# Split attention: ScalarE's work for coming heads and its copies of sums are queued behind a step's exp and its rounded transposed probabilities

## The chip, the cores and the metric

One core of a Trainium2 chip runs the whole program. The metric is the device time of one execution in microseconds (us). TensorE does the matrix products, VectorE, ScalarE and GpSimd the work on elements, and SyncE's queue starts the DMA transfers. In views of the profile they are PE (with PEld, its weight loads), DVE, ACT, POOL and SP. Every engine takes its own instructions strictly in the order of the program.

## The reference, cut to what matters

Attention over 4 sequences of 576 positions with 8 heads of 64, a causal window of 128 positions and a linear bias by distance, and then two MLPs on its output of 2304 tokens by 512:

```python
scores = scale * np.matmul(q, k.transpose(0, 1, 3, 2))
bias = slopes[:, None, None] * (-np.abs(rel).astype(np.float32))[None, :, :]
mask = (rel >= 0) & (rel < window)
scores = np.where(mask, scores + bias[None], -1000000000.0)
attn = np.exp(scores - np.max(scores, axis=-1, keepdims=True))
attn = attn / (np.sum(attn, axis=-1, keepdims=True) + 1e-09)
x = (attn @ v) as (2304, 512)
h = x @ w_in1; g = max(h, (clip(h, -1, 1) + 1)**2 / 4); x = g @ w_out1
h = x @ w_in2; g = h * clip(h + 3, 0, 6) / 6;           y = g @ w_out2
```

## The kernel before

Everything is in fp32, and most products are made from a rounded part and its remainder ("hi" and "lo"): two or three matrix products take the place of one. ScalarE makes the rounded part by a copy (`split_hi`, L152) and VectorE or GpSimd the remainder by a subtraction (`split_lo`, L159).

**Units, heads, steps.** The 2304 tokens are cut into 12 units of 64 to 256 tokens, and a unit has 8 heads, so there are 96 heads, numbered 0 to 95 here. A head has a step for every 128 of its query positions: heads of units with 192 or 256 tokens have two, those of units with 128 tokens one. Units 0 to 3 (heads 0 to 31) run in a plain form ("whole"), units 4 to 11 in the split form that the change is about. Of those, units 5, 7 and 11 have 128 tokens: heads 40 to 47, 56 to 63 and 88 to 95 have one step each, and the heads before them (32 to 39, 48 to 55, 80 to 87) have two.

**A step of split attention.** `stage_a` makes the scores in the one PSUM bank "s" (L411: `kh` and then `kl` against `qs`), overlays the two halves of the window (L438), adds the bias and takes the row's extreme (L441, VectorE), takes exp with its sum (L445, ScalarE), adds epsilon and inverts the sum (L448 and L449, VectorE), and scales (L450, GpSimd). `stage_b` comes three ticks later: a transpose by TensorE (L470), its rounded copy by ScalarE (L152 into `dist` or `tt`), the remainder (L483, VectorE) and two selections by GpSimd (L488). `stage_c`, five ticks after `stage_a`, multiplies with the values (L554), and adds up the halves of the result through ScalarE (`xf`, L152) and VectorE (L572). For odd heads `to_x` then makes the MLP's input `x` (L152 on ScalarE, L159 on VectorE).

**Preparing a head.** `prep(n)` turns the loaded keys and queries of head n into operands: `kh` (L389) and the first half of `qs` (L390) by ScalarE, then `kl` (L391) by VectorE from `kh`, and `qs` (L393) by GpSimd from ScalarE's `qs`; for even heads the values `vs` too. The first score product of head n needs `kh` and the finished `qs`, the second `kl`.

**The order.** `tick()` runs the late stages of earlier steps, then `stage_a` of its own, and then, under `behind()`, the `to_x` of finished pairs and `more_preps`: the step (n, 0) prepares head n+1 where head n has two steps and up to head n+2 where it has one. So head 39 (two steps) prepares 40, and head 40 (one step) prepares 41 and 42. Only SyncE's queue is in the order of the code. On the other engines the framework's scheduler chooses the order, and `tc.issue_after(op)` binds it: what is traced in such a block stands behind `op` on `op`'s own engine. `behind()` names three operations of VectorE: the last row reduction (L441), the last remainder of transposed probabilities (L483) and the last sum (L572). On ScalarE and GpSimd it binds nothing.

**The MLP between the steps.** The first MLP runs in the same stretch. For each of 16 chunks of a block, `first` is 12 matrix products of 256 or 384 tokens (h, L659), `activate` goes VectorE (L688), ScalarE (L689), VectorE (L690), ScalarE (`g`, L152), GpSimd (`g`, L159), and `second` is 12 more products (acc, L701), two chunks late. `run_block` calls `flush` (acc, and at a block's end `finish`, which copies the sums out) under `behind()` too. In wide blocks h has a single bank, so the next h waits for L690.

Of the kernel before, what the change touches and what calls it, by code (L numbers as in the profile page):

```python
# [15 lines left out]
AF = mybir.ActivationFunctionType  # L16
# [13 lines left out]
HI = dict(v="act", th="act", xf="act", x="act", g="act", x2="act")  # L30
# [10 lines left out]
def tile_window_attention_two_mlps(  # L41
# [15 lines left out]
    nc = tc.nc  # L57
# [7 lines left out]
    scale = 1.0 / math.sqrt(D)  # L65
# [55 lines left out]
    def keep_busy(bank, n):  # L121


        for a in range(0, n, 2 * P):
            nc.tensor.matmul(bank[:, a:a + 2 * P], zeros[:, :P], zeros, start=True, stop=True, skip_group_check=True)
# [23 lines left out]

    def split_hi(eng, hi, x):  # L150
        if eng == "act":
            nc.scalar.copy(hi, x)  # L152
        elif eng == "pool":
            nc.gpsimd.tensor_scalar(out=hi, in0=x, scalar1=1.0, scalar2=1.0, op0=ALU.mult, op1=ALU.mult)
        else:
            engines[eng].tensor_copy(hi, x)
# [6 lines left out]
    class Weights:  # L163
        def __init__(self, nm, w_in, w_out, pool, sign_pool):
            self.sign_pool = sign_pool
            self.src = {"i": w_in.bitcast(U32), "o": w_out.bitcast(U32)}
            self.nm, self.pool = nm, pool
            self.raw, self.m, self.hl = {}, {}, {}
            self.n_load = 0
            self.n_conv = 0  # L170
# [43 lines left out]
        def conv3(self, f):  # L214
            del self.raw[f]
            m = self.m.pop(f)
            hl = wpool.tile([P, 2, 2, PIECE], F32R, tag=f"w{f}", name=f"w{self.nm}{f}")
            split_hi("act", hl[:, 0], m)
            split_lo("dve", hl[:, 1], m, hl[:, 0])
            self.hl[f] = hl  # L220
# [27 lines left out]
    for j, (t0, n) in enumerate(units):  # L248
        for h in range(H):
            u = Head()  # L250
# [19 lines left out]
    class Attention:  # L270
        def __init__(self, raw, proc, work, xs):
            self.raw, self.proc, self.work, self.xs = raw, proc, work, xs
            self.n_load = self.n_prep = self.t = 0
            self.row, self.low, self.sum, self.late = None, None, None, []
            self.k_owners, self.v_owners = [], []

            self.vts = [raw.tile([P, KCH, 2 * D + 2], F32, tag="vr", name=f"vr{i}", bufs=3) for i in range(3)]

            kr = [raw.tile([P, 2, KMAX], F32, tag="kr", name=f"kw{i}") for i in range(2)]
            qr = [raw.tile([P, 2, UMAX], F32, tag="qr", name=f"qw{i}") for i in range(2)]  # L280
            self.kw = [t[:, j] for t in kr for j in range(2)]
            self.kw += [proc.tile([P, KMAX], F32, tag=tag, name=f"kw_{tag}{i}") for tag in ("kh", "kl") for i in range(2)]
            self.qw = [t[:, j] for t in qr for j in range(2)]
            self.pt = [work.tile([P, 2 * P], F32, tag="p", name=f"p{i}", bufs=LAG_B + 1) for i in range(LAG_B + 1)]
            a = next(h for h in range(H) if plain not in (h, h + 1))
            self.pt.append(dist[:, a:a + 2].bitcast(F32).rearrange("p a b -> p (a b)"))
            free = [h for h in range(a + 2, H) if h != plain]
            self.tc = [dist[:, h:h + 2].bitcast(F32R).rearrange("p a (s q) -> p a s q", s=1)[:, :, 0] for h in free[:4:2]]
            assert len(self.tc) == 2 and all(h + 1 in free for h in free[:4:2])
            self.near, self.takes = zeros[:, :P], zeros[:, P:]  # L290
            self.n_p = self.n_tc = 0
# [122 lines left out]
        def stage_a(self, n, i):  # L414

            u = heads[n]
            a, m = u.qbs[i]
            ks = a - P if a >= P else 0
            nk = a + m - ks
            qo, ko = a - u.q0, ks - u.k0  # L420
            bo = 0 if a >= P else P

            tag = ("s", "acc0", "acc1")[(n * 2 + i) % 3] if u.unit == 0 else "s"
            ps = psum.tile([P, BANK], F32, tag=tag, name=f"s{n}_{i}")
            u.n_a += 1
            if u.unit == 0:
                keep_busy(ps, 2 * P)
            self.scores(u, ps, qo, ko, nk)
            pt = self.pt[self.n_p % ((LAG_B if u.whole else LAG_B_SPLIT) + 1)]
            self.n_p += 1  # L430
            sm = self.work.tile([P, 4], F32, tag="sm", name=f"sm{n}_{i}", bufs=4)
            if m < P and u.whole:
                nc.gpsimd.memset(pt[:, nk:2 * P], 0.0)
            table = dist[:, u.h if u.whole else plain, bo:bo + nk]
            if not u.whole and a >= P:


                nc.vector.copy_predicated(out=ps[:, :m], mask=self.takes[:, :m].bitcast(U16), data=ps[:, P:P + m])  # L438
                nk, table = P, self.near

            self.row = nc.vector.tensor_tensor_reduce(  # L441
                out=pt[:, :nk], in0=ps[:, :nk], in1=table,
                scale=-scale if u.whole else -slopes[u.h],
                scalar=3.0e38, op0=ALU.add, op1=ALU.min, accum_out=sm[:, 0:1])
            nc.scalar.activation(out=pt[:, :nk], in_=pt[:, :nk], func=AF.Exp, bias=sm[:, 0:1],  # L445
                                 scale=-1.0, accum_out=None if u.whole else sm[:, 1:2])
            if not u.whole:
                nc.vector.tensor_scalar(out=sm[:, 2:3], in0=sm[:, 1:2], scalar1=EPS, scalar2=None, op0=ALU.add)  # L448
                nc.vector.reciprocal(sm[:, 3:4], sm[:, 2:3])  # L449
                nc.gpsimd.tensor_scalar(out=pt[:, :nk], in0=pt[:, :nk], scalar1=sm[:, 3:4], scalar2=1.0,  # L450
                                        op0=ALU.mult, op1=ALU.mult)
            u.p[i] = pt

        def stage_b(self, n, i):

            u = heads[n]
            a, m = u.qbs[i]
            has_prev = a >= P
            if i == 0:
                u.tt = self.work.tile([P, 2, 2 * QB, P], F32 if u.whole else F32R, tag="tt", name=f"tt{n}")  # L460
            pt = u.p.pop(i)
            bank = psum.tile([P, BANK], F32, tag=("t", "t2")[(n * 3 + i) % 2] if u.unit <= first_wide else "t",
                             name=f"t{n}_{i}")
            ps = bank.rearrange("p (s q) -> p s q", q=P)

            s0 = 2 * i if u.prev else 2 * i - 1
            assert has_prev or m == P
            if u.whole and has_prev:
                nc.tensor.transpose(ps[:, 0, :], pt[:, :P], ident)
            nc.tensor.transpose(ps[:, 1, :], pt[:, P:] if u.whole and has_prev else pt[:, :P], ident)  # L470
            if u.whole:
                c = 0 if has_prev else 1
                split_hi(HI["th"], u.tt[:, 0, s0 + c:s0 + 2, :], ps[:, c:2, :])
                return
            src = ps[:, 1, :m]
            if has_prev:
                both = self.tc[self.n_tc % len(self.tc)][:, :, :m]
                self.n_tc += 1
            else:
                both = u.tt[:, :, s0 + 1, :m]  # L480
            hi, lo = both[:, 0], both[:, 1]
            split_hi(HI["th"], hi, src)
            self.low = nc.vector.tensor_tensor(out=lo, in0=src, in1=hi.bitcast(F32), op=ALU.subtract)  # L483
            if has_prev:


                for s, sign in ((0, -1), (1, 1)):
                    nc.gpsimd.affine_select(out=u.tt[:, :, s0 + s, :m], in_=both, compare_op=ALU.is_ge, fill=0.0,  # L488
                                            base=-1 + s, pattern=[[0, 2], [sign, m]], channel_multiplier=-sign)
# [140 lines left out]
        def behind(self):  # L630


            stack = ExitStack()
            for op in (self.row, self.low, self.sum):
                if op:
                    stack.enter_context(tc.issue_after(op.ins))
            return stack
# [141 lines left out]
    class Chunks:  # L779
# [22 lines left out]
        def run(self, mlp, blk, f, part, x, between, after, behind=ExitStack):  # L802
            self.pend.append((mlp, blk, f, part, mlp.first(x, f, mlp.blocks[blk][1])))
            between()
            with behind():
                self.flush(mlp.lag)
            after()
# [540 lines left out]
```

## Time and profile before

| | before |
|---|---|
| median of 3 runs | 946.19 us (946.13 to 946.76) |
| the profiled execution | 946.02 us |
| its span in the trace | 944.3 us |
| PE busy | 928.5 us, 98% |
| DVE / ACT / POOL busy | 70% / 57% / 32% |

The span runs from the first instruction to the last; 1.7 us of the profiled execution lie around it. TensorE's granted clock is at its full level in every slice. Times of a row in the trace count from the start of the span. Split attention stands between about 120 us and 470 us; a busy TensorE is not TensorE at its peak, because the ends of its instructions are modelled, so a wait can also show as a later start of the next product.

### The profile page before, as it was taken

The page shows a single profiled execution, that of the slowest core. Times are in us where ns is not written, and L with a number is a line of the kernel's source. Part 1 is how long each engine was busy: PE and PEld are TensorE (multiplying, and loading weights), DVE is VectorE, ACT ScalarE, POOL GpSimd, SP SyncE. Part 2 cuts the span into 40 slices and gives each one's busy share as a digit, 9 for nine tenths or more (in the row PEclk, how much of TensorE's full clock was granted, in tenths as well). Part 3 has the DMA queues.
Part 4 walks back from the last instruction along what each step waited for, and adds up shares of the span by engine and source line. Part 5 has one row for each costly group of instructions (what it writes and reads, how often), then busy time and mean ns, then how long its engine had stood idle before and what let it go on. Part 6 is the DMA issues. An engine that isn't in the chain of part 4 may idle for free.

```text
span 944.3 us, 17237 instructions
## 1 busy us (share of the span) xinstructions
PE 928.5 (98%) x5683; PEld 875.5 (93%) x5683; DVE 659.4 (70%) x1750; ACT 535.6 (57%) x1349; POOL 306.8 (32%) x575
## 2 busy tenths in 40 slices
PE   8899999999999999999999999999999999999998
PEld 6799999999999999999999999999999888898987
DVE  6998975786677677767656899958557777644443
ACT  6998854676667566666635786535333334423233
POOL 3243845787668676777710000000000000000000
PEclk9999999999999999999999999999999999999999
DMA  8858322232222212322017771004264654543431
GB/s 256 240 178 264 111 89 88 68 86 67 73 64 72 79 46 62 89 75 62 1 55 270 266 237 55 1 23 167 81 210 170 232 174 146 169 124 114 123 112 67
DMA packets 95337, 114.90 MB, mean 122 GB/s; under 512 B 8848, under 2 KB 73616, under 8 KB 95248
## 3 DMA queue, kind: packets, MB, share of 16 engines
q1 hardware_dynamic: 95248, 113.80, 38.3%
q8 instruction: 45, 0.74, 0.3%
q14 instruction: 44, 0.36, 0.1%
HBM read 88.60 MB, written 25.17 MB: 120 GB/s over the span
## 4 chain that ended last, share of the span: by engine, by line
PE 89%; DVE 5%; ACT 2%; DMA 2%; issue 1%; POOL 1%; SPq 0%; ACTq 0%; DVEq 0%; POOLq 0%
PE h L659 26%; PE acc L760 21%; PE acc L701 18%; PE y L1249 7%; PE x L1249 5%; PE s L411 4%; PE r L554 3%; PE t L470 2%; PE r L506 2%; DMA rawa<-w_in 1%; DVE r L688 1%; DVE kl L391 1%; DVE r L690 1%; DVE x L159 1%; DMA kw<-kT 1%
## 5 line engine op out<-in xcount | busy, mean ns | idle before, releaser
L659 PE MATMUL h<-x,wa 128*128 128x384 f32 (+1 forms) x1344 | 231.0, 317 | 1.4 <-DVE r L690 0.9
L701 PE MATMUL acc<-g,wa 128*128 128x384 f32 (+1 forms) x1344 | 227.4, 315 | 0.4 <-POOL g L159 0.4
L760 PE MATMUL acc<-wb,g 128*128 128x512 f32 x861 | 222.2, 393 | 0.0
L659 PEld LDWEIGHTS h<-x,wa 128*128 128x128 f32 x1344 | 206.8, 189 | 4.3 <-DVE r L690 3.4
L701 PEld LDWEIGHTS acc<-g,wa 128*128 128x128 f32 x1344 | 206.3, 189 | 0.7 <-POOL g L159 0.6
L760 PEld LDWEIGHTS acc<-wb,g 128*128 128x128 f32 x861 | 159.4, 188 | 24.9
L152 ACT CAST g<-r 128x384 fp32r<-128x384 f32 (+1 forms) x208 | 101.6, 489 | 71.4 <-DVE r L1196 37.6
L159 POOL TENSOR_TENSOR g<-r,g 128x256 fp32r<-128x256 f32 (+1 forms) x96 | 92.5, 964 | 67.7 <-ACT g L152 54.8
L689 ACT ACTIVATE r<-r 128x384 f32<-128x384 f32 (+1 forms) x112 | 53.5, 479 | 81.3 <-DVE r L688 81.0
L159 DVE TENSOR_TENSOR g<-r,g 128x384 fp32r<-128x384 f32 x112 | 62.4, 557 | 41.9 <-ACT g L152 41.6
L688 DVE TENSOR_SCALAR r<-h 128x384 f32<-128x384 f32 (+1 forms) x112 | 55.4, 495 | 44.0 <-PE h L659 37.3
L488 POOL TENSOR_SCALAR_AFFINE_SELECT tt<-dist 128x256 fp32r<-128x256 f32 (+1 forms) x176 | 76.9, 458 | 13.9 <-DVE dist L483 13.8
L690 DVE TENSOR_TENSOR r<-h,r 128x384 f32<-128x384 f32 (+1 forms) x112 | 55.8, 499 | 30.3 <-ACT r L689 28.4
L659 PE MATMUL h<-x,wb 128*128 128x384 f32 x384 | 72.5, 336 | 0.0
L659 PEld LDWEIGHTS h<-x,wb 128*128 128x128 f32 x384 | 68.2, 188 | 2.6
L445 ACT ACTIVATE p<-p,sm 128x128 f32<-128x128 f32 (+2 forms) x134 | 57.3, 430 | 20.9 <-DVE sm L441 20.5
L1194 ACT ACTIVATE r<-u 128x384 f32<-128x384 f32 x32 | 16.9, 527 | 56.2 <-DVE u L1258 56.2
L554 PEld LDWEIGHTS r<-tt,vs 128*128 128x128 f32 x304 | 44.7, 189 | 3.2 <-issue 1.4
L393 POOL TENSOR_TENSOR qs<-qr,qs 128x256 fp32r<-128x256 f32 (+2 forms) x64 | 39.4, 616 | 24.9 <-ACT qs L390 13.3
L554 PE MATMUL r<-tt,vs 128*128 128x128 f32 (+3 forms) x304 | 44.3, 262 | 1.4 <-POOL tt L488 0.9
L470 PE MATMUL t<-ident,p 128*128 128x128 f32 x134 | 38.4, 288 | 0.5 <-ACT tt L152 0.5
L1249 PE MATMUL y<-wb,w 128*128 128x384 f32 x192 | 38.7, 336 | 0.0
(161 smaller groups left out, 1554.6 us busy)
## 6 DMA issues: line engine op xcount, KB each, us to landing
w<-wd SPq DMA_DIRECT2D x88, 256.0 KB, 2.7
rawa<-w_in SPq DMA_DIRECT2D x16, 512.0 KB, 5.3
rawa<-w_out SPq DMA_DIRECT2D x16, 512.0 KB, 5.4
rawb<-w_in SPq DMA_DIRECT2D x16, 512.0 KB, 3.8
rawb<-w_out SPq DMA_DIRECT2D x16, 512.0 KB, 4.7
wd<-sum SPq DMA_DIRECT2D x32, 256.0 KB, 2.1
wd<-wb SPq DMA_DIRECT2D x24, 256.0 KB, 2.8
out<-o SPq DMA_DIRECT2D x17, 256.0 KB, 2.3
```

The source lines that it names most:

```text
L152: nc.scalar.copy(hi, x)
L159: engines[eng].tensor_tensor(out=lo, in0=x, in1=hi.bitcast(F32), op=ALU.subtract)
L445: nc.scalar.activation(out=pt[:, :nk], in_=pt[:, :nk], func=AF.Exp, bias=sm[:, 0:1], scale=-1.0, accum_out=None if u.whole else sm[:, 1:2])
L470: nc.tensor.transpose(ps[:, 1, :], pt[:, P:] if u.whole and has_prev else pt[:, :P], ident)
L488: nc.gpsimd.affine_select(out=u.tt[:, :, s0 + s, :m], in_=both, compare_op=ALU.is_ge, fill=0.0, base=-1 + s, pattern=[[0, 2], [sign, m]], ...
L554: nc.tensor.matmul(u.r[:, qo:qo + nq], u.vs[:, j, c, :, :].rearrange("p a d -> p (a d)"), u.tt[:, part].rearrange("p s q -> p (s q)")[:, s ...
L659: nc.tensor.matmul(ps[:, :n], self.W.w_in(a, c, f), self.x_chunk(x, b, c, n), start=(k == 0), stop=(k == 3 * KC - 1))
L688: nc.vector.tensor_scalar(out=r[:, :n], in0=ps[:, :n], scalar1=-1.0, scalar2=1.0, op0=ALU.max, op1=ALU.min)
L690: self.larger = nc.vector.tensor_tensor(out=r[:, :n], in0=ps[:, :n], in1=r[:, :n], op=ALU.max)
L701: nc.tensor.matmul(acc[i][:, o * n:(o + 1) * n], self.W.w_out(a, f)[:, e * P:(e + 1) * P], g[:, b, :n], start=(first and k == 0 and o == 0 ...
L760: nc.tensor.matmul(acc[t][:, :DM], g[:, b, tg * P:(tg + 1) * P], self.W.w_out(a, f), start=(first and k == 0), stop=(last and k == 2))
L1249: nc.tensor.matmul(ps[:, :N2], w[:, a, c * P:(c + 1) * P], self.x.operand(k, c, b), start=(start and n == 0), stop=(n == 5), skip_group_ch ...
```

## The change

`split_hi` returns its copy, the exp of a split step and the rounded copy of the transposed probabilities are remembered as `self.exp` and `self.high`, and `behind()` names them too. Both are on ScalarE, so now ScalarE's part of all that is traced under `behind()` stands behind them: `kh`, `qs` and `vs` of coming heads, `x`, and the copies of sums in `finish`.

```diff
     def split_hi(eng, hi, x):
         if eng == "act":
-            nc.scalar.copy(hi, x)
+            return nc.scalar.copy(hi, x)
...
-            nc.scalar.activation(out=pt[:, :nk], in_=pt[:, :nk], func=AF.Exp, bias=sm[:, 0:1],
-                                 scale=-1.0, accum_out=None if u.whole else sm[:, 1:2])
+            exp = nc.scalar.activation(out=pt[:, :nk], in_=pt[:, :nk], func=AF.Exp, bias=sm[:, 0:1],
+                                       scale=-1.0, accum_out=None if u.whole else sm[:, 1:2])
+            if not u.whole:
+                self.exp = exp
...
-            split_hi(HI["th"], hi, src)
+            self.high = split_hi(HI["th"], hi, src)
...
             stack = ExitStack()
-            for op in (self.row, self.low, self.sum):
+            for op in (self.row, self.low, self.sum, self.exp, self.high):
                 if op:
                     stack.enter_context(tc.issue_after(op.ins))
             return stack
```

No instruction is added or taken away. What moves is the order on ScalarE, and, since the scheduler follows what is ready, on VectorE and GpSimd; SyncE's queue is the same, and TensorE's order differs in three places by a few rows. From L447 on, line numbers of the changed kernel are two higher.

First place: head 57, the second head of the one-step unit 7. On ScalarE, before (`kh_4211` and `qs_4213` belong to head 57, `kh_4218` to head 58, `p_115` and `dist ... sm_1_4168` are the exps of the two steps of head 55):

```order
L445 ACTIVATE p_115,sm_0_4121<-p_115,sm_0_4121 128x128
L152 CAST tt_4160<-t_0_4161 128x128
L389 ACTIVATE kh_4211<-kr_3933 128x256
L390 ACTIVATE qs_4213<-qr_3934,minus_odd 128x128
L689 ACTIVATE r<-r 128x384
L445 ACTIVATE dist,sm_1_4168<-dist,sm_1_4168 128x128
L152 CAST g<-r 128x384
L152 CAST vs_4134<-vr_103 128x2x64 x2
L152 COPY xf_4102<-r_4159 64x256
L152 CAST dist<-t_1_4193 128x128
L389 ACTIVATE kh_4218<-kr_4112 128x256
```

The same place of ScalarE in the changed kernel (`p_113,sm_0_4202` is the exp of head 56):

```order
L445 ACTIVATE dist,sm_1_4168<-dist,sm_1_4168 128x128
L152 CAST vs_4134<-vr_103 128x2x64 x2
L152 COPY xf_4102<-r_4159 64x256
L152 CAST dist<-t_1_4193 128x128
L445 ACTIVATE p_113,sm_0_4202<-p_113,sm_0_4202 128x128
L389 ACTIVATE kh_4211<-kr_3933 128x256
L152 CAST x<-xf_4102 128x256
L390 ACTIVATE qs_4213<-qr_3934,minus_odd 128x128
L389 ACTIVATE kh_4218<-kr_4112 128x256
L390 ACTIVATE qs_4220<-qr_4113,minus_odd 128x128
```

The preparation of head 57 has gone from ahead of the last exp of head 55 to behind the exp of head 56, with the cast of `x` between its two parts.

On GpSimd at the same place, before (the rows `p` and `dist` scale the probabilities of a step):

```order
L450 TENSOR_SCALAR p_115<-p_115,sm_0_4121 128x128
L393 TENSOR_TENSOR qs_4213<-qr_3934,qs_4213 128x128
L450 TENSOR_SCALAR dist<-dist,sm_1_4168 128x128
L159 TENSOR_TENSOR g<-r,g 128x384
L159 TENSOR_TENSOR vs_4134<-vr_103,vs_4134 128x2x64 x2
L488 AFFINE_SELECT tt_4160<-dist 128x2x128 x2
L450 TENSOR_SCALAR p_113<-p_113,sm_0_4202 128x128
L393 TENSOR_TENSOR qs_4220<-qr_4113,qs_4220 128x128
L393 TENSOR_TENSOR qs_4275<-qr_4113,qs_4275 128x128
```

And in the changed kernel:

```order
L452 TENSOR_SCALAR p_115<-p_115,sm_0_4121 128x128
L393 TENSOR_TENSOR qs_4129<-qr_3934,qs_4129 128x128
L159 TENSOR_TENSOR g<-r,g 128x384
L452 TENSOR_SCALAR dist<-dist,sm_1_4168 128x128
L159 TENSOR_TENSOR vs_4134<-vr_103,vs_4134 128x2x64 x2
L490 AFFINE_SELECT tt_4160<-dist 128x2x128 x2
L452 TENSOR_SCALAR p_113<-p_113,sm_0_4202 128x128
L393 TENSOR_TENSOR qs_4213<-qr_3934,qs_4213 128x128
L393 TENSOR_TENSOR qs_4220<-qr_4113,qs_4220 128x128
```

The finished queries of head 57 (`qs_4213`) now come behind the scaling of head 56. The heads 41 (`qs_2934`) and 89 (`qs_6907`) have gone the same way, from ahead of the last scalings of the heads before the unit to right behind the scaling of head 40 and of head 88.

Second place: TensorE at head 57, before (`s_0_4263` are its scores, `acc` the second product of the MLP):

```order
L659 MATMUL h<-x,wa_1002 128x384 x12
L470 MATMUL t_0_4259<-ident,p_115 128x128
L411 MATMUL s_0_4263<-kh_4211,qs_4213 128x256
L411 MATMUL s_0_4263<-kl_4212,qs_4213 128x256
L701 MATMUL acc_3883<-g,wa_739 128x384 x3
L701 MATMUL acc_3884<-g,wa_739 128x384 x3
```

And in the changed kernel:

```order
L661 MATMUL h<-x,wa_1002 128x384 x12
L472 MATMUL t_0_4259<-ident,p_115 128x128
L703 MATMUL acc_3883<-g,wa_739 128x384 x2
L411 MATMUL s_0_4263<-kh_4211,qs_4213 128x256
L411 MATMUL s_0_4263<-kl_4212,qs_4213 128x256
L703 MATMUL acc_3883<-g,wa_739 128x384
L703 MATMUL acc_3884<-g,wa_739 128x384 x3
```

Two products of the MLP have come ahead of the scores. At head 41 four stand ahead of the first score product and two more ahead of the second; at head 89 TensorE's order is unchanged.

Third place: VectorE at the first step of a two-step head of unit 8, before (`kl_5190` belongs to the head after it):

```order
L441 ISA p_115,sm_0_5182<-s_0_5179,zeros 128x128
L441 ISA sm_0_5182 128x1
L391 SCALAR_TENSOR_TENSOR kl_5190<-kr_4995,kh_5189 128x320
L448 TENSOR_SCALAR sm_0_5182<-sm_0_5182 128x1
L449 RECIPROCAL sm_0_5182<-sm_0_5182 128x1
L483 TENSOR_TENSOR dist<-t_0_5222,dist 128x128
```

And in the changed kernel:

```order
L441 ISA p_115,sm_0_5182<-s_0_5179,zeros 128x128
L441 ISA sm_0_5182 128x1
L450 TENSOR_SCALAR sm_0_5182<-sm_0_5182 128x1
L451 RECIPROCAL sm_0_5182<-sm_0_5182 128x1
L391 SCALAR_TENSOR_TENSOR kl_5190<-kr_4995,kh_5189 128x320
L485 TENSOR_TENSOR dist<-t_0_5222,dist 128x128
```

`kl` stood between the row reduction and the operation that needs the exp of the same step; now it stands behind both. That is so for 57 of the 64 `kl`.

## Rows read from the trace of the kernel before

**Rows 1.** The page: busy time of each engine over the span.

```profile
PE 928.5 (98%) x5683; PEld 875.5 (93%) x5683; DVE 659.4 (70%) x1750; ACT 535.6 (57%) x1349; POOL 306.8 (32%) x575
```

**Rows 2.** Busy time by stretch: us, busy PE, PEld, DVE, ACT, POOL, clock, DMA.

```profile
165.00:466.00 301.00, 297.95 (x2009) 291.65 (x2008) 217.68 (x833) 200.44 (x677) 221.91 (x448) 1.00 0.23 66
318.00:345.00 27.00, 26.25 (x164) 24.93 (x163) 20.55 (x78) 17.70 (x61) 20.17 (x48) 1.00 0.23 71
```

**Rows 3.** TensorE's longest wait from 165 to 466: total, times, longest.

```profile
PE r L554 <- POOL tt L488: 0.9, 1, 0.9
```

**Rows 4.** Timeline around head 57: start, us, engine, operation, [idle before <-releaser].

```profile
264.30 0.39 ACT L445 ACTIVATE p<-p,sm 128x128 f32<-128x128 f32 x1
264.69 0.40 ACT L152 CAST x<-xf 128x256 fp32r<-128x256 f32 x1
264.89 0.42 DVE L391 SCALAR_TENSOR_TENSOR kl<-kr,kh 128x256 fp32r<-128x256 f32 x1
...
265.21 0.36 PE L411 MATMUL s<-kh,qs 128*128 128x256 f32 x1
...
265.59 2.24 PE L701 MATMUL acc<-g,wa 128*128 128x384 f32 x12
265.65 0.42 ACT L389 ACTIVATE kh<-kr 128x256 fp32r<-128x256 f32 x1
...
265.97 0.39 ACT L390 ACTIVATE qs<-qr,minus_odd 128x128 fp32r<-128x128 f32 x1
266.10 0.53 POOL L450 TENSOR_SCALAR p<-p,sm 128x128 f32<-128x128 f32 x1
...
266.60 0.88 POOL L393 TENSOR_TENSOR qs<-qr,qs 128x128 fp32r<-128x128 f32 x2
...
268.07 0.61 PE L659 MATMUL h<-x,wa 128*128 128x384 f32 x2 [0.23 <-DVE r L690]
```

**Rows 5.** Timeline around head 89.

```profile
440.77 0.36 PE L411 MATMUL s<-kh,qs 128*128 128x256 f32 x1
...
441.06 0.79 POOL L450 TENSOR_SCALAR p<-p,sm 128x128 f32<-128x128 f32 x1
441.09 2.27 PE L701 MATMUL acc<-g,wa 128*128 128x384 f32 x12
...
441.81 0.46 POOL L393 TENSOR_TENSOR qs<-qr,qs 128x128 fp32r<-128x128 f32 x1
...
443.41 0.44 PE L659 MATMUL h<-x,wa 128*128 128x384 f32 x1
```

**Rows 6.** Timeline around head 41.

```profile
190.34 0.36 PE L411 MATMUL s<-kh,qs 128*128 128x256 f32 x1
...
190.88 0.39 PE L411 MATMUL s<-kl,qs 128*128 128x256 f32 x1 [0.17 <-DVE kl L391]
...
191.10 1.60 PE L701 MATMUL acc<-g,wa 128*128 128x256 f32 x12
...
192.20 0.37 POOL L450 TENSOR_SCALAR p<-p,sm 128x128 f32<-128x128 f32 x1
...
192.53 0.88 POOL L393 TENSOR_TENSOR qs<-qr,qs 128x128 fp32r<-128x128 f32 x2
192.53 1.60 PE L659 MATMUL h<-x,wa 128*128 128x256 f32 x12
```

**Rows 7.** VectorE's waits for exp from 165 to 466: total, times, longest.

```profile
DVE sm L448 <- ACT p L445: 11.8, 28, 0.9
DVE sm L448 <- ACT dist L445: 8.3, 17, 0.8
```

**Rows 8.** Timeline in unit 8: a remainder of keys beside GpSimd's `g`.

```profile
321.77 1.01 POOL L159 TENSOR_TENSOR g<-r,g 128x384 fp32r<-128x384 f32 x1
...
321.82 1.31 DVE L391 SCALAR_TENSOR_TENSOR kl<-kr,kh 128x320 fp32r<-128x320 f32 x1
```

More of the change, by code (lines that the diff above doesn't have):

```diff
@@ L273, in __init__ @@
             self.n_load = self.n_prep = self.t = 0
-            self.row, self.low, self.sum, self.late = None, None, None, []
+            self.row, self.low, self.sum, self.exp, self.high, self.late = None, None, None, None, None, []
             self.k_owners, self.v_owners = [], []
```

## The prediction

> **What bounds the kernel.** I read the page's busy times first. TensorE is busy 928.5 us of 944.3 [rows 1]. In the stretch where the change acts it is nearer still: from 165 to 466 us it is busy 297.95 of 301.00 us, while VectorE is busy 217.68, GpSimd 221.91 and ScalarE 200.44 [rows 2]. Three things follow. ScalarE, whose order changes, idles a third of that stretch. A gain can come only from the 3.05 us in which TensorE idles there. And any new wait of TensorE is paid in full, because the little idle time behind it is all that could take it up. TensorE's waits say the same: the longest kind is one wait of 0.9 us for a selection by GpSimd [rows 3]. The granted clock is 1.00 throughout, so no part of the sum is about the clock.
>
> So the question is not how much ScalarE's queue gains for exp, but whether something that TensorE needs at once now stands behind an exp. I looked for heads whose preparation is traced one step before its use, and then read the timeline around each.
>
> **Cost 1: three heads are prepared too late.** In a run of two-step heads, step (n, 0) prepares head n+1, whose scores come two steps later; standing behind exp of (n, 0) costs nothing, because a whole step lies between. In a run of one-step heads, n prepares n+2, with the same cover. But where the units change from two steps to one, the last two-step head prepares only the first one-step head, and that first one prepares the next two. Its own step is the one just ahead of their first use. So heads 41, 57 and 89 are prepared behind the exp of the step straight before them. Without the step that covers the others, everything costs what it costs there.
>
> Head 57. The exp of head 56 starts at 264.30 and takes 0.39, so ScalarE is free at 264.69. Now `kh`, `x` and `qs` follow, and the same kinds take 0.42, 0.40 and 0.39, so `qs` leaves ScalarE at 265.90. GpSimd scales head 56 at 266.10 and starts a pair of `qs` at 266.60; one of the pair is half of 0.88, so head 57's queries are finished at 267.04. Today its scores start at 265.21, and the two score products take 0.38 up to the first acc [rows 4]. In the new order two of the twelve acc (2.24 / 12 = 0.187 each) go ahead of them, and TensorE then waits, some 1.4 us. After 267.04 come the two scores, 0.38, and ten acc, 1.87: the next h can start at 269.29. Today it starts at 268.07, after a wait of 0.23 for L690, which the delay absorbs. **+1.2 us.** If GpSimd takes `qs` as soon as ScalarE delivers it (265.90 + 0.44 = 266.34), it is 0.5; if its queue is half a microsecond later than today, 1.7.
>
> Head 89. GpSimd starts the scaling of head 88 at 441.06, and a `qs` at 441.81 that takes 0.46. If that place goes to head 89, its scores start at 442.27, where today they start at 440.77. No acc has been moved ahead, so TensorE waits through it; twelve acc follow, and the next h, at 443.41 today, moves by as much [rows 5]. **+1.5 us**, with 0.4 as lower bound: if GpSimd let the `qs` run ahead of the 0.79 of the scaling, most of the wait would go.
>
> Head 41. The scaling of head 40 stands at 192.20 and the pair of `qs` behind it at 192.53; GpSimd's queue ahead of it loses one `qs` (0.44, half of the pair) to this place, so the scaling can come up to that much earlier. Head 41's queries are then finished between 192.53 and 192.97, and its scores start at 190.34 today. Four acc of 1.60 / 12 = 0.133 go ahead. Behind the wait come the first score product (0.2: start to start as above), two acc (0.27), the second product (0.2) and six acc (0.80): the next h is at 194.0 to 194.4, and today at 192.53 [rows 6]. I take the early end, **+1.5 us** (bounds 0.4, as for the other two, and 1.9).
>
> Sum of the three: 4.2 us. Of TensorE's 3.05 us of idle time some lies behind these places, in waits for work that does not move with TensorE, and so takes up part of the delay; I take 0.4 off, about half of the single longest wait [rows 3]. **+3.8 us**, bounds 1.3 - 0.4 = 0.9 and 1.7 + 1.5 + 1.9 = 5.1.
>
> **Cost 2: VectorE's waits.** Before, `kl` often ran between the row reduction and L448, so that VectorE did useful work while ScalarE made the exp. Now 57 of 64 `kl` stand behind L448 and L449, because `kh` comes behind the exp. VectorE waited 28 and 17 times for exp, 11.8 and 8.3 us, so 0.45 each [rows 7]. With 57 more such places VectorE would wait up to 57 x 0.45 = 26 us more. VectorE has 301.00 - 217.68 = 83 us idle in this stretch [rows 2], so nearly all is idle time that only changes place; that idle time is the cover, and where it is short the waits go to TensorE through the s bank or through L690, for which h waits. The tight place is 318 to 345, where VectorE is busy 20.55 of 27.00 us [rows 2]. I take +0.5 us, bounds 0 and 2.5 (a tenth of the 26). GpSimd takes its instructions in order too, and its `qs` of every head now waits for ScalarE's later `qs`; for the heads that are used a whole step later that costs nothing.
>
> **Parts that cost nothing.** The copies of sums in `finish` and `x` for odd heads have their next use steps later; the cover is that distance, and without it each would cost its 0.4 on the path. The gain, exps that no longer stand behind preparations, is at most the idle time of TensorE that hangs on an exp. VectorE's 20.1 us of waiting for exp [rows 7] is the visible part, and it lies inside VectorE's idle time, so I count 0 (bounds 0 and -3.05, all that TensorE idles).
>
> **Sum.** The profiled execution took 946.02 us (its span 944.3 and 1.7 around it), 0.17 under the median. 946.0 + 3.8 + 0.5 = **950.3 us**, the next h after the three places being late by as much to the end, since TensorE has no slack to catch up.
>
> **A rule against this.** The trace shows `kl` of 128x320 at 1.31 us where GpSimd's `g`, 1.01 us, started 0.05 earlier [rows 8], and a `kl` of 128x256 at 0.42 with little beside it [rows 4]. By columns the larger would take 0.42 x 320 / 256 = 0.53, so 0.8 is lost to the overlap. Moving `kl` may take it out of this overlap. The Trainium skill, page "SBUF — State Buffer", section "Who interferes with whom", says that a VectorE instruction with two inputs in SBUF contends with a GpSimd instruction that reads SBUF, and that the one that comes second is blocked fully, not slowed. The 1.31 in this trace agrees. What it would give is the first rival.
>
> **The rivals.**
>
> *Faster: `kl` leaves the overlap with `g`.* For the eight heads of the stretch around 318 to 345, 8 x 0.8 = 6 us of VectorE would come free. TensorE can take from it only what it idles: 0.75 us from 318 to 345, and 3.05 in all [rows 2]. For it to decide, the three late heads must be covered and this must exceed 1.9 us: 943.0 to 944.3. For it speaks the 1.31; against it, VectorE idles already. With smaller late heads it only trims the forecast. Together with an exp that comes sooner: chance 0.14.
>
> *No change.* GpSimd or ScalarE has more room than the timeline shows and the late heads cost 0.5 each, part of which the 0.23 at L690 and the 0.9 wait absorb: 946 to 948. For it: the 0.23 at head 57. Against it: at 41 and 89 h starts with no wait, so nothing is there to absorb. That the order does not really change is excluded by the places shown. Chance 0.22.
>
> *Slower yet: VectorE's wait becomes the bound.* If a fifth of the 26 us reaches TensorE, +5 and the 3.8: 952 to 955. It decides where VectorE's next reduction, held in order behind a waiting L448, releases the s bank later than TensorE wants it. Against it: 83 us of idle time. Chance 0.06.
>
> *The forecast*, 948.1 to 952: chance 0.58.
>
> **How the numbers follow.** 0.2% of 946, 1.9 us, is about what a measurement of this kernel can tell from no change. Slower by more: 0.58 + 0.06 = 0.64; same 0.22; faster 0.14. The likeliest case is 950.3, its own range 948.1 to 952. The range that should hold 8 in 10 reaches from 944.2, which leaves out most of the faster case, to 953.0, which holds the upper bounds 946 + 5.1 + 0.5 and part of the worst rival.
>
> **What would show it.** After the change TensorE should show three waits at L411 for GpSimd's `qs` (L393), of 1 to 1.7 us each, near 190, 265 and 441 us. Its idle time from 165 to 466 should be 6 to 8 us where it is 3.05. VectorE's waits for exp (then L450) should be 30 to 45 us where they are 20.1, with no new TensorE wait on `kl` or on the s bank that sums to a microsecond. The prediction is wrong if no wait stands at the three heads, if TensorE's idle time falls under 3 us, or if the waits are there and the time lost at each is taken up before the next h.

## The result and the profile after

The changed kernel takes 952.86 us (median of 6 runs, 951.68 to 953.60), the kernel before 946.86 us beside it (6 runs, 946.13 to 947.95). The ratio is 1.0062, with a 95% interval of 1.0049 to 1.0075: slower by 6.0 us, inside the forecast range and over its value by 2.6. The profiled execution took 953.6 us; its span is 951.9.

The page's busy times and the two stretches of [rows 1, 2], in the changed kernel:

```profile
PE 931.5 (98%) x5683; PEld 877.3 (92%) x5683; DVE 655.2 (69%) x1750; ACT 537.4 (56%) x1349; POOL 303.0 (32%) x575
```

```profile
165.00:466.00 301.00, 293.95 (x1965) 286.97 (x1965) 208.15 (x812) 198.46 (x660) 214.42 (x437) 0.99 0.23 66
318.00:345.00 27.00, 26.39 (x167) 25.16 (x167) 19.21 (x82) 18.38 (x62) 20.31 (x46) 1.00 0.23 71
```

TensorE idles 7.05 us of the 301 where it idled 3.05; 6 to 8 were forecast. VectorE, ScalarE and GpSimd are less busy in this window, in part because it holds fewer of their instructions (812 where there were 833 on VectorE); over the whole span VectorE and GpSimd also take less time for the same instructions (655.2 against 659.4 us, and 303.0 against 306.8). Two more things have changed: TensorE's busy time has grown by 3.0 us (931.5 against 928.5) for the same 5683 instructions, and the granted clock of the stretch is 0.99, where it was 1.00. The clock, shown below, can account for 1.7 of the 3.0. But free3, a run below, also has 931.1 us, at a clock of 1.00: part of a loss can show as busy time, because the ends of TensorE's instructions are modelled.

TensorE's waits from 165 to 466 us, which answer to [rows 3] (total, times, longest):

```profile
PE s L411 <- POOL qs L393: 4.3, 5, 1.4
PE r L556 <- POOL tt L490: 0.8, 1, 0.8
PE h L661 <- DVE r L692: 0.8, 2, 0.4
```

The wait for selections is the old one. The wait for `qs` is new and now the largest: five times, where three were forecast. The timeline around head 57, as in [rows 4] (the program is about 3 us later here than before):

```profile
267.09 0.40 ACT L445 ACTIVATE p<-p,sm 128x128 f32<-128x128 f32 x1
...
267.49 0.40 ACT L389 ACTIVATE kh<-kr 128x256 fp32r<-128x256 f32 x1
...
267.80 0.39 ACT L152 CAST x<-xf 128x256 fp32r<-128x256 f32 x1
...
268.10 0.40 ACT L390 ACTIVATE qs<-qr,minus_odd 128x128 fp32r<-128x128 f32 x1
...
268.25 0.60 PE L703 MATMUL acc<-g,wa 128*128 128x384 f32 x2
...
268.91 0.53 POOL L452 TENSOR_SCALAR p<-p,sm 128x128 f32<-128x128 f32 x1
...
269.41 1.05 POOL L393 TENSOR_TENSOR qs<-qr,qs 128x128 fp32r<-128x128 f32 x2
...
269.91 0.38 PE L411 MATMUL s<-kh,qs 128*128 128x256 f32 x1 [1.06 <-POOL qs L393]
```

It is the forecast row by row: exp, then `kh`, `x` and `qs` on ScalarE, the scaling and then `qs` on GpSimd, two acc ahead of the scores, and TensorE waiting. The waits at heads 41 and 89 are 1.43 us at 193.07 and 1.05 us at 448.11. VectorE's waits for exp, which answer to [rows 7]:

```profile
DVE sm L450 <- ACT p L445: 28.1, 51, 0.8
DVE sm L450 <- ACT dist L445: 9.6, 18, 0.8
```

That is 37.7 us in place of 20.1, in the 30 to 45 that were forecast.

The two waits for `qs` that nobody forecast stand at heads 68 and 75, in units whose heads all have two steps. Around head 68 in the changed kernel:

```profile
321.11 0.40 ACT L445 ACTIVATE p<-p,sm 128x128 f32<-128x128 f32 x1
...
321.50 0.46 ACT L389 ACTIVATE kh<-kr 128x320 fp32r<-128x320 f32 x1
...
321.87 0.44 ACT L390 ACTIVATE qs<-qr,minus_odd 128x192 fp32r<-128x192 f32 x1
...
322.35 0.60 POOL L452 TENSOR_SCALAR p<-p,sm 128x128 f32<-128x128 f32 x1
...
322.89 0.15 POOL L395 MEMSET qs<- 128x64 f32 x1
...
323.00 0.58 POOL L393 TENSOR_TENSOR qs<-qr,qs 128x192 fp32r<-128x192 f32 x1
...
323.64 0.39 PE L411 MATMUL s<-kh,qs 128*128 128x256 f32 x1 [0.45 <-POOL qs L393]
```

The head has a step of cover, and it isn't enough: from exp to the finished `qs` it takes 2.5 us, because ScalarE makes `kh` first and GpSimd scales the probabilities first, and the second step of a 192-token head is only 64 positions long.

At head 75 the same happens, and then something else. The granted clock (the column before the last two) by stretches of two microseconds, changed kernel:

```profile
360.00:362.00 2.00, 1.22 (x9) 0.83 (x7) 1.58 (x8) 1.36 (x6) 1.95 (x4) 1.00 0.00 0
362.00:364.00 2.00, 1.67 (x11) 1.48 (x12) 1.28 (x8) 1.05 (x5) 1.33 (x5) 0.98 0.22 61
364.00:366.00 2.00, 2.00 (x8) 2.00 (x7) 0.59 (x3) 1.07 (x4) 1.28 (x4) 0.50 0.36 98
366.00:368.00 2.00, 2.00 (x11) 1.90 (x10) 1.51 (x6) 0.92 (x3) 0.15 (x1) 0.67 0.51 148
```

For some 3 us the clock is 0.50, the lower level (1.2 GHz where 2.4 is full). What TensorE did before it:

```profile
361.47 0.77 PE L556 MATMUL r<-tt,vs 128*128 128x192 f32 x4 [0.78 <-POOL tt L490]
362.07 0.33 PE L472 MATMUL t<-ident,dist 128*128 128x128 f32 x1
362.74 0.33 PE L411 MATMUL s<-kh,qs 128*128 128x128 f32 x1 [0.33 <-POOL qs L393]
```

The wait of 0.78 is the one that the kernel before has too [rows 3]; the 0.33 for `qs` 1.3 us behind it is new. After both, TensorE ran at half its speed. The three rows below 1.00 lose 1.7 us of the full clock, which over a span of 951.9 us makes a mean of 0.998. In the changed kernel's six runs the mean is 0.998 in two (953.60 and 952.98), 0.999 in three (952.62, 952.97 and 952.75) and 1.000 in one, the fastest (951.68). A mean of 0.999 is no sign of such a fall: four traces below have it (recip_kl, rest, both, kh_only), and their clock falls only in the last few microseconds of the span, behind the last product; the runs of the kernel before that were taken beside the experiments have 0.999 or 1.000. So the fall is seen in the profiled run, and its sign in two runs of six. The median of the other four is 952.7, 5.8 us over before.

### The profile page after: what moved, and what is told of

Its sections match the earlier page's. It is cut to its first block, busy times and chain, and to the rows that moved or that the text cites. A ratio compares the mean times of both kernels' runs of the same rounds, so it can differ in the third digit from the quotient of the medians.

```text
span 951.9 us, 17222 instructions
## 1 busy us (share of the span) xinstructions
PE 931.5 (98%) x5683; PEld 877.3 (92%) x5683; DVE 655.2 (69%) x1750; ACT 537.4 (56%) x1349; POOL 303.0 (32%) x575
## 4 chain that ended last, share of the span: by engine, by line
PE 79%; DVE 7%; ACT 5%; DMA 3%; issue 3%; POOL 2%; SPq 0%; ACTq 0%; POOLq 0%; DVEq 0%
PE h L661 22%; PE acc L762 21%; PE acc L703 15%; PE y L1251 7%; PE x L1251 5%; PE s L411 3%; PE r L556 2%; PE r L508 1%; PE t L472 1%; DVE r L690 1%; DVE r L692 1%; ACT p L445 1%; DVE kl L391 1%; ACT r L691 1%; DMA rawa<-w_in 1%
## 5 line engine op out<-in xcount | busy, mean ns | idle before, releaser
L159 POOL TENSOR_TENSOR g<-r,g 128x256 fp32r<-128x256 f32 (+1 forms) x96 | 90.0, 938 | 90.0 <-ACT g L152 63.9
L690 DVE TENSOR_SCALAR r<-h 128x384 f32<-128x384 f32 (+1 forms) x112 | 55.3, 494 | 37.7 <-PE h L661 34.3
L490 POOL TENSOR_SCALAR_AFFINE_SELECT tt<-dist 128x256 fp32r<-128x256 f32 (+1 forms) x176 | 73.6, 440 | 12.7 <-DVE dist L485 11.5
L450 DVE TENSOR_SCALAR sm<-sm 128x1 f32<-128x1 f32 x104 | 15.9, 153 | 41.6 <-ACT p L445 30.3
L411 PE MATMUL s<-kh,qs 128*128 128x256 f32 (+1 forms) x104 | 36.6, 352 | 5.0 <-POOL qs L393 4.3
```

Source lines behind the costliest of these rows:

```text
L159: engines[eng].tensor_tensor(out=lo, in0=x, in1=hi.bitcast(F32), op=ALU.subtract)
L411: nc.tensor.matmul(ps[:, :nk], q[:, qo:qo + P], k[:, ko:ko + nk], start=(w == 0), stop=(w == len(parts) - 1))
L690: nc.vector.tensor_scalar(out=r[:, :n], in0=ps[:, :n], scalar1=-1.0, scalar2=1.0, op0=ALU.max, op1=ALU.min)
```

## The experiments

All of them edit `behind()` so that each place chooses what is named. Times are medians, and the kernel before is the one run on the same chip. In the diffs, minus lines are the changed kernel's.

**late3 and free3.** In late3 only the steps of heads 40, 56 and 88, which prepare the late heads, bind ScalarE's work (`flush` doesn't); free3 is the complement. The last line is free3's.

```diff
-            for op in (self.row, self.low, self.sum, self.exp, self.high):
+            for op in (self.row, self.low, self.sum) + ((self.exp, self.high) if more else ()):
...
-                with self.behind():
+                with self.behind(n in (40, 56, 88)):
+                with self.behind(n not in (40, 56, 88)):
```

> Only the steps of heads 40, 56 and 88 bind ScalarE's work behind exp and the rounded probabilities; everything else is in the order of before. If the three late heads cost what the trace of the changed kernel shows there (the delay that stays a few steps later is 0.7, 0.7 and 1.0 us), the time is 2.4 us over before, and by the working of the prediction 3.8 over it; TensorE waits for qs at heads 41, 57 and 89, 1.0 to 1.5 us each. If the late heads were the whole loss, it would be 6 us over before. If the loss came from the other heads alone, it would be at the time of before.

late3: 949.26 against 946.60 us, ratio 1.0030 (1.0019 to 1.0041), so 2.7 us. Its waits:

```profile
PE s L411 <- POOL qs L393: 3.6, 3, 1.5
PE r L556 <- POOL tt L490: 0.9, 1, 0.9
```

Three waits, as in the theory, 3.6 us of waiting for 2.7 of time. The late heads are a loss by themselves, and not the whole one.

> The complement: the changed kernel, but the steps of heads 40, 56 and 88 bind as in the kernel before. If the late heads cost 2.4 us, this stands 3.5 us over before and 2.4 under the changed kernel, and no wait for qs of over 0.5 us is left; the rest is then VectorE's and GpSimd's lateness at two-step heads and the granted clock. If the late heads were the whole loss, it stands at the time of before. If they were no part of it, at that of the changed kernel.

free3: 952.12 us, ratio 1.0053 (1.0040 to 1.0065). It did not come down by 2.4 us, as the theory had it, but by 0.7 at the median. Its five runs fall into two groups: 950.12 and 950.96 at a mean clock of 1.000, and 952.12 to 953.02 at 0.998. The first two stand 3.9 us over before, where the changed kernel's runs without the sign of the clock's fall stand 5.8 over: like with like, it came down by 1.9. So there is a loss outside the late heads that is larger than theirs, and the clock adds about 2 us to it in some runs.

**early.** Heads 41, 57 and 89 are prepared one step earlier.

```diff
                         self.more_preps(n + 1 if u.whole or len(u.qbs) > 1 else n + 2)
+                    elif n + 1 in (40, 56, 88):
+                        self.more_preps(n + 2)
```

> The changed kernel, with heads 41, 57 and 89 prepared one step earlier, behind the second step of heads 39, 55 and 87. If the cover of a step is what those heads lack, the result is as in free3: 2 to 3 us under the changed kernel, and no wait for qs at the three heads. If the loss there came from GpSimd being busy and not from the place behind exp, the waits of about 1 us stay and the time is that of the changed kernel.

950.93 us, ratio 1.0044 (1.0031 to 1.0057): 1.9 us under the changed kernel's median, though the two intervals overlap. Without the run at 0.998 it stands 4.0 us over before, where the changed kernel stands 5.8: a gain of 1.8. TensorE's waits for `qs`:

```profile
PE s L411 <- POOL qs L393: 0.8, 2, 0.5
```

They stand at heads 68 and 75; at the three late heads there is none. The missing step of cover was the cause of the waits there.

**recip and recip_kl.** ScalarE is bound by nothing; VectorE's reciprocal takes the place of exp in the list. In recip_kl only the preparations are bound so, and `x` and the copies of sums as before.

```diff
-                nc.vector.reciprocal(sm[:, 3:4], sm[:, 2:3])
+                self.recip = nc.vector.reciprocal(sm[:, 3:4], sm[:, 2:3])
...
-            for op in (self.row, self.low, self.sum, self.exp, self.high):
+            for op in (self.row, self.low, self.sum) + ((self.recip,) if more else ()):
```

> The kernel before, in which VectorE's reciprocal takes the place of exp in the list: ScalarE is bound by nothing, but VectorE's kl and x stand behind the reciprocal of the step, as most of them do in the changed kernel. If VectorE's order is what costs the part of the loss that is not at the three heads, this stands 1.5 to 3 us over before and VectorE's waits for exp grow from 20 us to 35 to 40. If that part comes from GpSimd's late qs or from the clock, it stands within 0.5 us of before.

recip: 950.39 us, ratio 1.0039 (1.0027 to 1.0052), 3.8 us. VectorE's waits for exp:

```profile
DVE sm L450 <- ACT p L445: 27.6, 49, 0.9
DVE sm L450 <- ACT dist L445: 7.7, 17, 0.8
```

That is 35.3 us, nearly the changed kernel's 37.7, with ScalarE free. The 3.8 us are more than the 1.5 to 3 that I expected. VectorE's order can cost as much as I gave to the late heads. "Alone" would be too much: the scheduler also moved some 20 of ScalarE's 1349 instructions and 13 of GpSimd's 575. None of it shows as one large wait: TensorE has nine waits there that share 4.4 us, where the kernel before has seven that share 2.3. The longest:

```profile
PE r L556 <- POOL vs L159: 0.9, 1, 0.9
```

> Like recip, but only the preparations (kl) stand behind the reciprocal; x and the copies of sums are bound as before. If kl's place alone makes the loss of VectorE's order, it stands 3 to 4 us over before, as recip does. If the x and the copies of sums do, it stands within 1 us of before, and the 0.46 us that TensorE waited for a copy of sums in recip is gone with the rest of the loss.

recip_kl: 948.61 against 946.76 us, ratio 1.0021 (1.0012 to 1.0030), 1.9 us, between the two cases that I expected. About half of recip's loss is `kl`; the other half comes when `x` and the copies are bound too. The wait of 0.5 us for a copy of sums (L726) is gone with it.

**both.** recip and late3 in one kernel.

> The edits of recip and of late3 in one kernel: VectorE's kl and x behind the reciprocal everywhere, ScalarE bound only at the steps of heads 40, 56 and 88. If VectorE's order (3.8 us in recip) and the late heads (2.7 us in late3) are two losses that account for the change, this stands 5 to 6.5 us over before, like the changed kernel. If one hides the other, as free3 suggests, it stands 4 to 4.5 us over before.

951.59 us, ratio 1.0056 (1.0043 to 1.0068), 4.8 us, between the two cases again. The losses don't add up: the late heads add about 1.0 us to recip (4.8 against 3.8), where they cost 2.7 alone. One wait that recip has, 0.6 us for `kl` at head 41, isn't there any more: the longer wait for `qs` takes its place.

**rest and rest2.** Preparations as before; only `x` and the copies of sums stand behind exp and the rounded probabilities.

```diff
                 with self.behind():
                     for x in late:
                         self.to_x(*x)
+                with self.behind(False):
                     if i == 0:
```

> The changed kernel, but preparations are bound as before: only x and the copies of sums stand behind exp and the rounded probabilities. By the prediction these parts cost nothing: within 0.5 us of before. If x and the copies are part of VectorE's loss, 1 to 3 us over before.

> The kernel of rest once more: preparations bound as before, x and the copies of sums behind exp and the rounded probabilities. It stood 0.66 us under before, with an interval that holds 1. If that is a gain, it shows again (0.4 to 0.9 us under); if it is scatter, it stands within 0.3 us of before.

946.10 against 946.76, and 946.35 against 946.75: ratios 0.9994 (0.9985 to 1.0003) and 0.9996 (0.9988 to 1.0005). These parts cost nothing while the preparations go ahead of them, as forecast. Whether they gain is open: both intervals hold 1, but the repeat's 0.40 lies at the lower edge of what I had named as a gain, and in their traces the stretch from head 38 to head 95 is 0.6 and 0.7 us shorter than in the one trace of before.

**high.** Only the rounded transposed probabilities are named.

> Only the rounded transposed probabilities are named, exp is not. They stand earlier in a step than exp, so kh and qs come 0.5 to 1 us earlier than in the changed kernel. If the place behind exp is what hurts, this loses half of it or less: 0 to 3 us over before, with TensorE's wait for qs at heads 41 and 57 under 0.7 us. If any binding of ScalarE to a step costs the same, it stands 5 to 6 us over before.

951.14 us, ratio 1.0046 (1.0032 to 1.0059), four of five runs at a clock of 0.998; the one at 1.000 took 949.61. I expected waits under 0.7 us at the late heads. They are there in full (4.2 us in four waits, the longest 1.5), and VectorE's waits for exp are 25.3 us. So it is not exp as such that makes the late heads late: to be bound to the rounded probabilities is enough. Most of VectorE's loss is gone here (9 of 64 `kl` stand behind the reciprocal, where it is 61 in the changed kernel), and the one run without the clock's fall stands 2.9 us over before, about late3's loss.

**kh_only, qs_only, kh_qs.** The late heads are prepared as before; at all others one of ScalarE's two operations, or both, stand behind exp and the rounded probabilities. `vs`, `x` and the copies are bound as before.

```diff
-            nc.scalar.activation(out=u.kh[:, :nk], in_=u.kr[:, :nk], func=AF.Copy, scale=unit)
+            with self.behind(self.hold, ()): nc.scalar.activation(out=u.kh[:, :nk], in_=u.kr[:, :nk], func=AF.Copy, scale=unit)
```

> At all heads but the late ones, only kh stands behind exp and the rounded probabilities, and with it kl on VectorE; qs, vs, x and the copies of sums are bound as before, and the heads 41, 57 and 89 are prepared as before. If kl's new place on VectorE is the larger part of the loss that free3 still has (3.9 us in its two runs at the full granted clock), this stands 2 to 4 us over before; by recip_kl it is 1.9. TensorE should have no wait for qs at 323 and 362 us, and every run should be at a granted clock of 0.999 or more. If kl costs nothing here, it stands at before.

kh_only: 947.61 against 946.75 us, ratio 1.0010 (1.0001 to 1.0019), 0.9 us, all runs at 0.999 or more. That is under the 2 to 4 us that I expected: `kl` is not the larger part of what free3 loses.

> The same for qs alone: ScalarE's qs, and so GpSimd's, stand behind exp; kh and kl are made as before. If GpSimd's qs come too late at some two-step heads too, TensorE waits for them at about 323 and 362 us (0.45 and 0.33 us in the changed kernel), the time is 1 to 2.5 us over before, and some runs show the granted clock of 0.998 that free3's slower runs show. If a whole step covers qs, as the prediction had it, it stands within 0.5 us of before and no run falls under 0.999.

qs_only: 948.00 us, ratio 1.0016 (1.0007 to 1.0025), 1.3 us; three of eleven runs at a clock of 0.997 or 0.998, and the other eight still 1.2 over before. TensorE waits for `qs` 0.17 us at head 68 and 0.34 at head 75. Its profiled execution is one of the three:

```profile
360.00:362.00 2.00, 1.69 (x7) 1.69 (x8) 1.51 (x8) 1.44 (x7) 1.37 (x5) 0.67 0.19 56
362.00:364.00 2.00, 2.00 (x8) 2.00 (x7) 0.16 (x1) 0.14 (x1) 0.93 (x2) 0.50 0.36 102
364.00:366.00 2.00, 2.00 (x13) 1.97 (x13) 1.48 (x6) 1.12 (x4) 0.15 (x1) 0.97 0.35 105
```

The clock falls at the same place in the program, with nothing bound otherwise than before but `qs`.

> kh_only and qs_only in one kernel: at all heads but the late ones, kh and qs stand behind exp; vs, x and the copies of sums are bound as before. If the losses add up, it stands 2.1 us over before (0.86 and 1.25), and what free3 has beyond that comes from vs, x and the copies standing in the same place. If kh and qs hold each other up (one queues behind the other, and both behind exp), it stands 3.5 to 5.5 us over before like free3, with the waits for qs at 323 and 362 us and the granted clock of 0.998 in some runs.

kh_qs: 949.85 against 946.96 us, ratio 1.0028 (1.0018 to 1.0038), 2.9 us, seven of nine runs at 0.998. The two at 1.000 (948.95 and 948.54) stand 1.8 us over before: at the full clock the two losses about add up. free3 has 3.9 at the full clock, so some 2 more come when `vs`, `x` and the copies stand in the same queue. These are two runs against two; the traces, up to the step ahead of the clock's fall (column 74,1 below), show 0.9 more. Which of the three it is was not separated.

**Where TensorE loses.** From the traces, the start of the first score product of a step, less that in the trace of before and less the difference at the second step of head 38 (which takes out what the executions differ by before), in us. "74,1" is the second step of head 74; the last column is the last head:

```
head           40     43     56     58    74,1    76     88     90     95
late3         0.00   1.13   1.29   2.05   2.00   2.02   1.98   2.92   2.92
early        -0.01   0.09   2.13   2.30   1.96   4.11   4.67   4.51   4.51
recip         0.48   1.17   1.91   2.00   1.86   2.13   2.41   2.45   2.72
qs_only       0.00   0.00   0.29   0.33   0.40   2.54   2.05   2.05   2.05
kh_qs         0.00   0.40   1.04   1.10   0.98   3.17   3.24   3.17   3.17
free3         0.00   0.39   2.26   2.25   1.91   2.51   2.85   2.77   2.77
changed       0.00   0.74   2.47   3.24   2.92   5.08   5.48   6.45   6.45
```

The changed kernel's 6.45 us fall into four parts. The late heads, from 40 to 43, from 56 to 58 and from 88 to 90: 0.74 + 0.77 + 0.97 = 2.5. The two-step heads from 43 to 56, where late3 loses 0.16 and free3 1.87: 1.7. From 74 to 76: 2.2, where free3, whose profiled execution kept its clock, loses 0.6 and kh_qs and qs_only, whose clock fell, 2.2 and 2.1; so 1.6 is the clock and 0.6 the late `qs`. What is left, 0.1, is small gains and losses elsewhere. Behind the start of head 95's scores the changed kernel loses another 0.6, of which a wait of 0.40 for VectorE's sum (L574) is the part that shows; with the 0.6 by which its trace was late ahead of the split part, that makes the 7.6 us between the two spans. One trace stands behind each row, so single tenths are not to be relied on.

## Why the prediction was right, and where it wasn't

**What bounds the kernel** was read rightly: TensorE has no slack, and what delays it is kept to the end (in late3 the delay is 2.05 us behind head 57 and 1.98 thirty heads later).

**Cost 1, the late heads**, was the right mechanism at the right three places, and the size was too high: 3.8 us forecast, 2.7 in late3, 2.5 in the changed kernel's trace; taken away from the changed kernel they give back 1.8 in the runs of early and 1.9 in its trace; the losses don't add up. I took 0.4 off for waits that stand behind and absorb; the waits are 3.6 us in late3 for 2.7 of time, so 0.9 is absorbed. My sums were made to the next h, and there heads 41, 57 and 89 of the changed kernel are late by 1.3, 0.9 and 1.1 us where I had 1.5, 1.2 and 1.5; a few steps on 0.7, 0.8 and 1.0 are left.

**Cost 2, VectorE's waits**, is the term that was mis-sized: "+0.5 us, bounds 0 and 2.5". The waits for exp came as forecast, but that nearly all of it "is idle time that only changes place" did not hold. With `kh`, and so `kl`, bound behind exp the loss is 0.9 us (kh_only), with `kl` behind the reciprocal 1.9 (recip_kl), and with `x` and VectorE's copies there too 3.8 (recip). VectorE idles 83 us of the stretch [rows 2], but the loss is spread over many short waits of TensorE (nine in recip). I read this so, without having shown it apart: an engine that takes its instructions in order can't use idle time that comes later, so each wait for exp pushes what stands behind it on VectorE, and a few steps have no room for that. I took the mean over the stretch, and the loss is made at the steps without room. In the changed kernel 1.7 us are lost between heads 43 and 56, where recip loses 0.7, kh_qs 0.6 and free3 1.9: there VectorE's part, by recip, is less than half, and the rest comes only when `vs`, `x` and the copies stand behind exp together with the preparations. What it is that they hold up there was not found.

**"For the heads that are used a whole step later that costs nothing"** failed at heads 68 and 75. A whole step is there, but TensorE waits 0.45 and 0.33 us, and qs_only is 1.3 us slower with nothing but `qs` bound behind exp.

**"No part of the sum is about the clock"** failed in the profiled run and, by the mean of 0.998, in one more of the six. It was true of the kernel before, and the change itself made the wait behind which the clock falls. That is worth 1.6 us where it happens.

So 3.8 + 0.5 was forecast, and 2.5 + 2.4 + 1.6 is what the trace has: the late heads, the other heads (1.7, 0.6 and 0.1) and the clock, with 0.6 more behind head 95. At the median of the runs it is 6.0, and 5.8 without the runs that show the clock's fall. The range held by luck: the first term was too large and the others too small, and 952.86 is 0.14 us from its upper end, outside the 948.1 to 952 that I gave to the forecast itself.

**The rivals.** *No change* and *faster* fell. The overlap that the faster one rested on did go, but it was smaller than I had it: only three of the eight `kl` of 128x320 stood beside a `g` (1.31, 1.14 and 1.31 us), the other five took 0.50 to 0.89, and I had put 0.8 us on all eight. In the changed kernel none stands beside a `g`. Together, before and after (busy us and mean ns of one):

```profile
L391 DVE SCALAR_TENSOR_TENSOR kl<-kr,kh 128x320 fp32r<-128x320 f32 x8 | 7.1, 892 | 0.0
```

```profile
L391 DVE SCALAR_TENSOR_TENSOR kl<-kr,kh 128x320 fp32r<-128x320 f32 x8 | 4.5, 560 | 0.1
```

2.6 us of VectorE came free, and TensorE lost time all the same, since VectorE wasn't the bound there. The rule of the Trainium skill (page "SBUF — State Buffer", section "Who interferes with whom") speaks of these instructions, and the shorter `kl` agrees with it. *VectorE's wait becomes the bound* deserved more than the 0.06 I gave it: the measured time lies in its 952 to 955, though not by its mechanism, for TensorE has no wait of over 0.2 us on the s bank. Its 5 us are too much, but recip's 3.8 us are more than the late heads cost.

No kernel here is shown to beat the kernel before: rest, the best, stands 0.66 and 0.40 us under it, and by its intervals can't be told from it.

## What to carry to other kernels

To queue preparation behind urgent work on one engine also moves all that follows from it on other engines, and there the order is strict too: here the copies on ScalarE were a part of the matter, and the subtraction on VectorE that used to fill the wait for exp was another. Ask of each moved operation how long the whole chain to its use is, not how many steps lie between, and look for the shortest step. An engine's idle time summed over a stretch does not show that a wait is covered: look whether the steps around that wait have it.

## What was unexpected of the hardware

TensorE's clock fell to half for about 3 us in a kernel that keeps it busy 98% of the span, behind two short waits close together (0.8 to 1.0 us for selections, 0.3 us for `qs`), and each time at the same place, between the first step of head 75 and the next head. Five traces show it (the changed kernel, early, high, qs_only and kh_qs), and from step 74,1 to head 76 they lose 2.1 to 2.3 us where free3 loses 0.6: it cost 1.5 to 1.7 us each time. That the two waits bring it about is not certain: free3's profiled execution has the same two (0.80 and 0.33 us) at a clock of 1.00 throughout, while three of its other runs show 0.998. The same place in that trace:

```profile
362.00:364.00 2.00, 1.67 (x10) 1.55 (x10) 1.00 (x7) 1.33 (x6) 1.33 (x5) 1.00 0.27 74
364.00:366.00 2.00, 2.00 (x14) 1.97 (x14) 1.50 (x6) 1.38 (x6) 1.08 (x4) 1.00 0.28 82
```

Nor is idle time alone the cause: the waits at heads 41 and 89, 1.43 and 1.05 us, are longer and left the clock at 1.00. What decides it is open.
